# Loads of a decode kernel divided over two hardware DMA queues, SP's and ACT's

## The chip, the core and the metric

The kernel runs on one core of a Trainium2 chip. The metric is the device time of one execution in microseconds (us); the time before is the median of three runs. A core has TensorE (PE), VectorE (DVE), ScalarE (ACT), GpSimd (POOL) and SyncE (SP), which run their own instruction streams in order and meet through semaphores, and 16 DMA engines that move data between HBM and the on-chip memory. A load is issued by an instruction on one of the engines and joins the queue that belongs to this engine: SP's is named q1 in the profile, ACT's q10.

## The reference

One token passes through grouped-query attention with a long cache, and then through a small MLP block. B = S = 1, D = 512, 32 query heads, 8 key/value heads, 16,384 cached positions, head dimension 128; all in bfloat16.

```python
def _A_ref(x, k_cache, v_cache, wq, wo):
    q = heads(x @ wq)                      # 32 heads of 128
    k = jnp.repeat(k_cache, 4, axis=1)     # 8 groups, 4 query heads each
    v = jnp.repeat(v_cache, 4, axis=1)
    scores = jnp.einsum("bhqd,bhkd->bhqk", q, k) * (Dh ** -0.5)
    p = _softmax(scores, axis=-1)
    o = jnp.einsum("bhqk,bhkd->bhqd", p, v)
    return merge(o) @ wo

def _B_ref(x, w1, w2, w3, w4):
    ...
    x1 = x + hs                            # hs is zero with one position
    h2 = _gelu(_layernorm(x1, axis=-1) @ w3) @ w4
    return x1 + h2

h = x + _A_ref(_layernorm(x, axis=-1), A_k_cache, A_v_cache, A_wq, A_wo)
h2 = h + _B_ref(_layernorm(h, axis=-1), B_w1, B_w2, B_w3, B_w4)
return h2
```

In the MLP block the reference shifts four quarters of a hidden row by one or two positions, fills with zeros and multiplies by w2. With a single position nothing but zeros is left, so hs is zero and the kernel doesn't load w1 and w2: after the attention it normalises h, normalises that again for the product with w3, and adds h, the normalised h and the product with w4.

What must be read is 79.17 MB: wq and wo (4.19 MB each), K and V of 8 groups (4.19 MB each per group), w3 and w4 (1.84 MB each).

## The kernel before

The author's small scheduler (class `Program`) takes operations in program order, notes for each which keys it reads and writes, and derives the semaphore waits. It does not reorder: the order of calls is the order on each engine. So an operation that is added to an engine stands behind everything that was recorded for this engine earlier.

Positions are laid out with 128 rows of 128 positions, so one group's K is a tile of 128 partitions x 32 KB (`kb`, two buffers), and V comes as two halves of 8,192 positions, each 128 x 16 KB (`vb`, three buffers; the halves of the last group go to the first K buffer). wq and wo share one buffer (`wqo`), and w3 and w4 go to the second K buffer once the last keys have been read.

The main loop (L461) runs over g = 0 to 8 and works on the keys of group g and the values of group g-1:

- `transpose_keys` (L374): VectorE transposes the K tile in 8 pieces into `kt`. Every piece takes from both halves of each row, so it needs the whole row.
- `scores` (L384): TensorE multiplies `kt` by the queries into `s_ps`, in two halves.
- `values` (L439): TensorE multiplies the weights of group g-1 by the value halves into `O_ps`. It comes between the two halves of the scores and after them.
- `max_a`, `max_b`, `max_c` (L395 to L418): the row maximum, then ScalarE's two exponentials (L414).
- `weights` (L422): TensorE transposes the exponentials, VectorE copies them to `pt`. `gather` (L451): VectorE copies `O_ps` to `o_sb`, TensorE adds it up in `A_ps`.
- then the loads for later: `load_v(g, 0)`, `load_v(g, 1)`, and `load_k(g + 2)` (L490 to L494), and in the last group the pieces of wo, w3 and w4 (L495 to L504).

All these loads are issued by SP, which does nothing else; only x is issued by ACT. In the loop a load is recorded after the exponentials of its group, but on SP it waits only for its own buffer: `load_k(g + 2)` for the 8 transposes of group g, `load_v` for the products of the half that was in the buffer three halves earlier. wq, K0 and K1 are issued ahead of the loop, and the two halves of V0, whose buffers are free, stand right behind them on SP.

After the loop: the sums are normalised (L509 to L516), 32 x 4 products with wo give h (L522), `row_sums` and the inverse roots run on VectorE, 16 products with w3 (L535), Gelu on ScalarE (L542), a transpose, 56 products with w4 (L555), the final sum (L559) and the store.

The text calls the whole key tile of a group K0 to K7, and v00, v01, v10, ... the halves of the values (group, half); wo0, w30, w40 and so on are the pieces of the last weights, as the code names them.

Of the kernel before, what the change touches and what calls it, by code (L numbers as in the profile page):

```python
# [117 lines left out]
NCH = D // 128  # L118
FQ = FM // 4
NHC = FM // 128  # L120
WO = ((0, 14), (14, 28), (28, 32))
W3 = ((0, 3), (3, 4))
W4 = ((0, 10), (10, 14))
KRING = 2
VRING = 3
VT = 64 * DH
# [4 lines left out]
def bass_sequential_preLN__gqa_block_cached__mixer_s_mlp__decode_kernel(  # L131
# [13 lines left out]
    with ExitStack() as ctx:  # L145
        sb = lambda name, shape, dt: ctx.enter_context(nc.sbuf_tensor(name, shape, dt))
        ps = lambda name, shape, dt: ctx.enter_context(nc.psum_tensor(name, shape, dt))
        P = Program(nc, ctx)
# [10 lines left out]
        x4 = sb("x4", [4, 128], BF16)  # L159
# [39 lines left out]
        wqo = sb("wqo", [128, NCH * HQ * DH], BF16)  # L199
        kb = [sb(f"kb{i}", [128, 128 * DH], BF16) for i in range(KRING)]  # L200
        kt = sb("kt", [128, 128 * DH], BF16)
        vb = [sb(f"vb{i}", [128, VT], BF16) for i in range(VRING)]
        w3_sb = kb[1][:, 0:NCH * FM].rearrange("p (k f) -> p k f", k=NCH)
        w4_sb = kb[1][:, NCH * FM:2 * NCH * FM].rearrange("p (m c) -> p m c", m=NHC)
# [6 lines left out]
        m_ps, n_ps = mn_ps[:, 0:256], mn_ps[:, 256:512]  # L211


        def load(name, dst, src, key, by="SP", also=()):
            P.op(by, lambda e: e.dma_start(dst, src), w=[key, *also], dma=name)  # L215

        def load_k(g):
            i = g % KRING
            load(f"k{i}", kb[i][:, :], A_k_cache[0, g].rearrange("(p t) d -> p (t d)", p=128), ("k", i, 0),
                 also=[("k", i, n) for n in range(1, 4)])  # L220

        def value_tile(g, A):

            if g == HKV - 1:
                return kb[0][:, A * VT:(A + 1) * VT], ("k", 0, A)
            i = (2 * g + A) % VRING
            return vb[i][:, :], ("v", i)

        def load_v(g, A):
            src = A_v_cache[0, g, A * 8192:(A + 1) * 8192, :].rearrange("(p t) d -> p (t d)", p=128)  # L230
            dst, key = value_tile(g, A)
            load("v" + "_".join(map(str, key[1:])), dst, src, key)


        def dve(fn, r=(), w=(), bank=()):
            return P.op("DVE", fn, r, w, bank)
# [36 lines left out]
        def inverse_root(i, n):  # L273
# [17 lines left out]
            for k in range(3):  # L291
# [4 lines left out]
                    r=[(S, 8 + n), (T, n)], w=[key])  # L296


        load("x4", x4[:, :], A_x[0, 0:1, :].rearrange("o (q j) -> (o q) j", q=4), "x4", "ACT")
        load("wq", wqo[:, :], A_wq.rearrange("(p k) c -> p (k c)", k=NCH), ("wo", 0),  # L300
             also=[("wo", n) for n in range(1, len(WO))])
        load_k(0)
        load_k(1)

# [6 lines left out]
        for b in range(2):  # L311
            for e_ in range(2):
                n = 2 * b + e_
# [7 lines left out]
            r=["ident"], w=["quarter"])  # L321
# [7 lines left out]
            r=["hT", (("st", 0), 0), (("st", 0), 6)], w=["xn"])  # L329
# [3 lines left out]
            r=["selq_f"], w=["selq"])  # L333
        dve(lambda e: e.memset(nscale[:, :], -SCALE), w=["nscale"])
        act(lambda e: e.activation(scr[0:1, 0:1], mean4[0:1, 0:1], ACTF.Exp), r=["mean4"], w=["scr"])
        for i in range(2):
# [5 lines left out]
            r=["ident_f"], w=["row32"])  # L342
        dve(lambda e: e.tensor_reduce(row4[:, :], row32[:, :].rearrange("p (a u h) -> p u h a", a=4, u=2)[:, 0, :, :], AX.X, ALU.add),
            r=["row32"], w=["row4"])
        dve(lambda e: e.tensor_reduce(maskdd[:, :], ident_f[:, :].rearrange("p (n d) -> p d n", d=4), AX.X, ALU.add),
            r=["ident_f"], w=["maskdd"])
# [3 lines left out]
            r=["row32"], w=["zo"])  # L350
# [4 lines left out]
        for h in range(HQ):  # L355
            for k in range(NCH):
                pe(lambda e, h=h, k=k: e.matmul(n_ps[:, h:h + 1],  # L357
                                                wqo[:, k * HQ * DH + h * DH:k * HQ * DH + (h + 1) * DH],
                                                xn[:, k:k + 1], start=(k == 0), stop=(k == NCH - 1)),
                   r=["xn"] + [("wo", n) for n in range(len(WO))], w=["n"], bank=["mn"])  # L360
        dve(lambda e: e.tensor_copy(QT[:, :], n_ps[:, 0:HQ]), r=["n"], w=["QT"], bank=["mn"])
# [4 lines left out]
        for a in range(4):  # L366
            lo, hi = 32 * a, 32 * a + 32
# [6 lines left out]
        def transpose_keys(g, ts):  # L374
            i = g % KRING
            for t in ts:
                view = lambda x, t=t: x[:, :].bitcast(I32).rearrange("p (x l w) -> p x (l w)", x=2, l=64)[
                    :, :, t * 512:(t + 1) * 512]
                dve(lambda e, i=i, view=view: e.transpose(view(kt), view(kb[i])),  # L379
                    r=[("k", i, n) for n in range(4)], w=[("kt", t)])  # L380

        ktv = kt[:, :].rearrange("p (x l b s e) -> p b e l x s", x=2, l=64, b=2, s=32, e=2)

        def scores(g, half):  # L384
            for n in range(4):
                for ct in range(4):
                    c8 = 4 * half + ct
                    pe(lambda e, g=g, half=half, n=n, ct=ct, c8=c8: e.matmul(  # L388
                        s_ps[32 * ct:32 * ct + 32, half, :],
                        qb[:, n, g, :, :, :].rearrange("p a u h -> p (a u h)"),  # L390
                        ktv[:, n // 2, n % 2, 8 * c8:8 * c8 + 8, :, :],
                        start=(n == 0), stop=(n == 3)),
                       r=["qb", ("kt", c8)], w=[("s", half)], bank=[("s", half)])

        def max_a(half):  # L395
            dve(lambda e: e.tensor_reduce(mx[:, half:half + 1], s_ps[:, half, :], AX.X, ALU.max),  # L396
                r=[("s", half)], w=[("mx", half)], bank=[("s", half)])
# [41 lines left out]
        def values(g, A, qs):  # L439
            tile, key = value_tile(g, A)  # L440
            for q in qs:
                for ct in range(4):
                    n = 32 * (q // 2) + 8 * ct + 4 * (q % 2)
                    pe(lambda e, q=q, ct=ct, n=n: e.matmul(  # L444
                        O_ps[g % 2][32 * ct:32 * ct + 16, :],
                        pt[g % 2][:, ct, A, 4 * q:4 * q + 4, :].rearrange("p l h -> p (l h)"),
                        tile[:, n * DH:(n + 4) * DH],
                        start=(A == 0 and q == 0), stop=(A == 1 and q == 3)),
                       r=[key, ("pt", g % 2)], w=[("O", g % 2)], bank=[("O", g % 2)])
# [11 lines left out]
        for g in range(HKV + 1):  # L461
            if g < HKV:
                transpose_keys(g, range(3 if g == 1 else 0, 4))
                scores(g, 0)
                transpose_keys(g, range(4, 6))
                max_a(0)
                transpose_keys(g, range(6, 8))
            if g:
                values(g - 1, 0, range(4))
            if g < HKV:  # L470
                scores(g, 1)
                max_a(1)
            if g == 0:
                transpose_keys(1, range(0, 1))
            if g:
                values(g - 1, 1, range(2))
            if g < HKV:
                max_b()
            if g:
                values(g - 1, 1, range(2, 4))  # L480
            if g < HKV:
                max_c(g)
            if g == 0:
                transpose_keys(1, range(1, 3))
            if g < HKV:
                weights(g)
                denominator(g)
            if g:
                gather(g - 1)
            if g < HKV:  # L490
                for A in range(2):
                    load_v(g, A)
                if g + 2 < HKV:
                    load_k(g + 2)  # L494
            if g == HKV - 1:  # L495
                for n, (lo, hi) in enumerate(WO):
                    load(f"wo{n}", wqo[:, lo * D:hi * D], A_wo.rearrange("(p r) c -> p (r c)", p=128)[:, lo * D:hi * D],
                         ("wo", n))
                w3_in = B_w3.rearrange("(p k) f -> p k f", p=128)
                for n, (lo, hi) in enumerate(W3):  # L500
                    load(f"w3{n}", w3_sb[:, lo:hi, :], w3_in[:, lo:hi, :], ("k", 1, n))
                w4_in = B_w4.rearrange("(p m) c -> p m c", p=128)
                for n, (lo, hi) in enumerate(W4):
                    load(f"w4{n}", w4_sb[:, lo:hi, :], w4_in[:, lo:hi, :], ("k", 1, 2 + n))  # L504
                act(lambda e: e.activation(scr[0:1, 1:2], mean4[0:1, 0:1], ACTF.Gelu_apprx_tanh),
                    r=["mean4"], w=["scr"])

# [7 lines left out]
            r=["o_m"], w=["o_f"])  # L515
# [3 lines left out]
           r=["quarter", "x4"], w=[("O", 0)], bank=[("O", 0)])  # L519
        for r_ in range(32):  # L520
            for q in range(4):
                pe(lambda e, r_=r_, q=q: e.matmul(O_ps[0][32 * q:32 * q + 32, 0:128], copies(o_b[:, r_:r_ + 1], 32),  # L522
                                                  wqo[:, r_ * D + q * 128:r_ * D + (q + 1) * 128],
                                                  start=False, stop=(r_ == 31), skip_group_check=True),
                   r=["o_b", ("wo", piece(WO, r_))], w=[("O", 0)], bank=[("O", 0)])
        s = st[1]
# [3 lines left out]
            r=["hT", (S, 0)], w=["hc"])  # L530


        for k in range(NCH):
            for q in range(4):
                pe(lambda e, k=k, q=q: e.matmul(s_ps[32 * q:32 * q + 32, 0, 0:FQ], hc[:, k, :],  # L535
                                                w3_sb[:, k, q * FQ:(q + 1) * FQ], start=(k == 0), stop=(k == NCH - 1)),
                   r=["hc", ("k", 1, piece(W3, k))], w=[("s", 0)], bank=[("s", 0)])
        variance(1)
        inverse_root(1, 1)
        for n in range(2):  # L540
            lo, hi = n * NHC // 2, (n + 1) * NHC // 2
# [9 lines left out]
            r=["hr", (S, 0), (S, 6)], w=["xs"])  # L551
        dve(lambda e: e.tensor_tensor(xsum[:, :], hr[:, :], xs[:, :], ALU.add), r=["hr", "xs"], w=["xsum"])
        for m in range(NHC):
            for o in range(4):
                pe(lambda e, m=m, o=o: e.matmul(  # L555
                    n_ps[32 * o:32 * o + 32, 0:128], hcol[:, m, :], w4_sb[:, m, o * 128:(o + 1) * 128],
                    start=(m == 0), stop=(m == NHC - 1)),
                   r=[("hcol", 2 * m // NHC), ("k", 1, 2 + piece(W4, m))], w=["n"], bank=["mn"])
        dve(lambda e: e.tensor_tensor(fin[:, :], xsum[:, :], n_ps[:, 0:128], ALU.add),  # L559
            r=["n", "xsum"], w=["fin"], bank=["mn"])  # L560
        P.op("SP", lambda e: e.dma_start(out[0, 0:1, :].rearrange("o (q j) -> (o q) j", q=4), fin[0:128:32, :]),
             r=["fin"], w=["out"], dma="out")
# [32 lines left out]
```

## Time and profile before

| | us |
|---|---|
| time, median of three runs | 194.05 (194.0 to 194.56) |
| the profiled execution's own time | 194.11 |
| its span on the core | 192.3 |
| TensorE busy, of the span | 112.5 (58%) |
| VectorE busy | 122.0 (63%) |
| ScalarE busy | 16.9 (9%) |
| SP's queue waiting for TensorE (before it issues) | 93.4 |
| SP's queue waiting for VectorE | 54.6 |
| K, from issue to landing, median | 26.3 |
| V half, from issue to landing, median | 24.2 |

The span is what the profiler saw between the first and the last instruction of the core; the time also holds what lies around it. Busy time counts an engine's instructions without waits and without the issue of transfers. In the page's slices each digit is the busy share of a fortieth of the span in tenths, and the GB/s row below it is what all queues moved in that slice. In a timeline row the columns are start and duration in us, engine, line, operation, result and operands with partitions x elements, and count; the bracket gives the idle time of the engine before it and what ended it.

### The profile page before, as it was taken

The numbers are of one execution on the slowest core, as the hardware profiler recorded it, in microseconds if no ns is written. First come the engines' busy times: TensorE is split into PE (matmuls) and PEld (weight loads), VectorE is DVE, ScalarE is ACT, GpSimd is POOL, SyncE is SP. The second block draws the span as 40 slices with busy tenths as digits, with TensorE's granted clock in tenths as the row PEclk, the third lists the DMA queues.
The fourth block names the chain that finished last, engine by engine and source line by source line (L and its number), as shares of the span: only waits on it lengthen the run. The fifth ranks groups of instructions, "written<-read, shape, count | busy, mean of one in ns | idle before, by whom it ended". The sixth has DMA issues, their size and how long they took to land.

```text
span 192.3 us, 2624 instructions
## 1 busy us (share of the span) xinstructions
PE 112.5 (58%) x1106; PEld 56.3 (29%) x1106; DVE 122.0 (63%) x236; ACT 16.9 (9%) x38; POOL 3.3 (2%) x17
## 2 busy tenths in 40 slices
PE   1025046567837766774776558645885676594533
PEld 1025001242234235223422522242223422453402
DVE  5834099499449928964894379536944796403274
ACT  3000000030030030003000200030003000600010
POOL 2000000000000000000000000000000000000000
PEclk9999999999985695588559655975558559669555
DMA  6999999999999999999999999999999999999990
GB/s 225 429 436 433 436 436 426 423 455 436 395 429 467 436 388 429 460 423 409 426 436 436 419 423 436 443 426 416 450 441 399 416 429 436 417 421 424 421 376 34
DMA packets 4634, 79.32 MB, mean 412 GB/s; under 512 B 528, under 2 KB 528, under 8 KB 912
## 3 DMA queue, kind: packets, MB, share of 16 engines
q1 hardware_dynamic: 4616, 79.17, 96.8%
q8 instruction: 8, 0.13, 0.3%
q14 instruction: 2, 0.02, 0.0%
q10 hardware_dynamic: 8, 0.00, 0.0%
HBM read 79.17 MB, written 0.00 MB: 412 GB/s over the span
## 4 chain that ended last, share of the span: by engine, by line
DMA 47%; DVE 18%; issue 2%; PE 2%; SPq 1%; ACT 0%; DVEq 0%; ACTq 0%
DMA kb<-in_A_k_cache_dram 28%; DMA wqo<-in_A_wo_dram 19%; DVE kt L379 13%; PE O_ps L522 1%; DVE mx L396 1%; DVE st L293 1%; SPq L215 1%; DVE hcol L546 1%; DVE sti L295 0%; PE T_ps L424 0%; DVE pt L430 0%; PE mn_ps L260 0%; ACT hg L542 0%; DVE xs L550 0%; DVE st L295 0%
## 5 line engine op out<-in xcount | busy, mean ns | idle before, releaser
L379 DVE STREAM_TRANSPOSE kt<-kb 128x1024 int32<-128x1024 int32 x64 | 74.0, 1212 | 11.1 <-DMA kb<-in_A_k_cache_dram 11.0
L388 PE MATMUL s_ps<-kt,qb 128*32 128x512 bf16 x256 | 47.7, 557 | 32.0 <-DVE kt L379 32.0
L444 PE MATMUL O_ps<-vb,pt 128*16 128x512 bf16 x224 | 29.2, 533 | 0.0
L388 PEld LDWEIGHTS s_ps<-kt,qb 128*32 128x32 bf16 x256 | 10.7, 114 | 61.6 <-DVE kt L379 53.9
L414 ACT ACTIVATE p_sb<-s_ps,bias 128x512 bf16<-128x512 f32 x16 | 12.7, 822 | 149.9 <-PE mn_ps L408 113.8
L456 PE MATMUL A_ps<-o_sb,zo 128*128 128x128 f32 x64 | 15.7, 422 | 10.5 <-DVE o_sb L453 10.5
L430 DVE COPY pt<-T_ps 64x256 bf16<-64x256 bf16 (+2 forms) x40 | 9.8, 261 | 15.5 <-PE T_ps L424 15.2
L396 DVE TENSOR_REDUCE mx<-s_ps 128x1 f32<-128x512 f32 x16 | 10.8, 677 | 11.9 <-PE s_ps L388 9.8
L424 PE MATMUL T_ps<-ident,p_sb 128*128 128x128 bf16 x128 | 11.7, 249 | 11.0 <-ACT p_sb L414 11.0
L456 PEld LDWEIGHTS A_ps<-o_sb,zo 128*128 128x128 f32 x64 | 13.4, 311 | 11.6 <-DVE o_sb L453 11.6
L424 PEld LDWEIGHTS T_ps<-ident,p_sb 128*128 128x128 bf16 x128 | 8.8, 111 | 12.9 <-ACT p_sb L414 12.7
L444 PEld LDWEIGHTS O_ps<-vb,pt 128*16 128x16 bf16 x224 | 9.4, 115 | 10.0 <-issue 8.5
L357 PE MATMUL mn_ps<-xn,wqo 128*128 128x1 bf16 x128 | 3.6, 165 | 9.4 <-DMA wqo<-in_A_wq_dram 9.4
L401 PE MATMUL mn_ps<-ident_f,mx 128*1 128x128 f32 x32 | 7.3, 322 | 2.5 <-DVE mx L396 2.5
L453 DVE COPY o_sb<-O_ps 128x512 f32<-128x512 f32 x8 | 5.5, 692 | 5.0 <-PE O_ps L444 4.7
L357 PEld LDWEIGHTS mn_ps<-xn,wqo 128*128 128x128 bf16 x128 | 3.5, 104 | 9.4 <-issue 9.4
L404 DVE TENSOR_REDUCE nm<-mn_ps 1x4 f32<-1x256 f32 x8 | 3.3, 406 | 3.7 <-PE mn_ps L401 3.7
L522 PE MATMUL O_ps<-wqo,o_b 128*32 128x128 bf16 x128 | 3.1, 271 | 2.9 <-DMA wqo<-in_A_wo_dram 1.6
L420 POOL COPY p_sb<-p_sb 128x64 bf16<-128x64 bf16 x8 | 1.9, 237 | 160.5 <-ACT p_sb L414 160.5
L401 PEld LDWEIGHTS mn_ps<-ident_f,mx 128*1 128x1 f32 x32 | 2.3, 90 | 7.5 <-DVE mx L396 5.3
L408 PEld LDWEIGHTS mn_ps<-nm,nscale 1*128 1x128 f32 x16 | 2.5, 198 | 5.5 <-DVE nm L404 5.5
L408 PE MATMUL mn_ps<-nm,nscale 1*128 1x4 f32 x16 | 3.2, 270 | 1.2 <-DVE nm L404 0.9
(75 smaller groups left out, 51.7 us busy)
## 6 DMA issues: line engine op xcount, KB each, us to landing
kb<-in_A_k_cache_dram SPq DMA_DIRECT2D x8, 4096.0 KB, 26.3
vb<-in_A_v_cache_dram SPq DMA_DIRECT2D x14, 2048.0 KB, 24.2
wqo<-in_A_wq_dram SPq DMA_DIRECT2D x1, 4096.0 KB, 12.3
kb<-in_A_v_cache_dram SPq DMA_DIRECT2D x2, 2048.0 KB, 26.8
wqo<-in_A_wo_dram SPq DMA_DIRECT2D x2, 1792.0 KB, 34.7
kb<-in_B_w_dram SPq DMA_DIRECT2D x1, 1344.0 KB, 22.9
kb<-in_B_w_dram SPq DMA_DIRECT2D x1, 1280.0 KB, 26.2
wqo<-in_A_wo_dram SPq DMA_DIRECT2D x1, 512.0 KB, 37.4
```

Of the source, the lines that this page charges most:

```text
L357: pe(lambda e, h=h, k=k: e.matmul(n_ps[:, h:h + 1], wqo[:, k * HQ * DH + h * DH:k * HQ * DH + (h + 1) * DH], xn[:, k:k + 1], start=(k == 0 ...
L379: dve(lambda e, i=i, view=view: e.transpose(view(kt), view(kb[i])), r=[("k", i, n) for n in range(4)], w=[("kt", t)])
L388: pe(lambda e, g=g, half=half, n=n, ct=ct, c8=c8: e.matmul(s_ps[32 * ct:32 * ct + 32, half, :], qb[:, n, g, :, :, :].rearrange("p a u h -> ...
L396: dve(lambda e: e.tensor_reduce(mx[:, half:half + 1], s_ps[:, half, :], AX.X, ALU.max), r=[("s", half)], w=[("mx", half)], bank=[("s", half)])
L401: pe(lambda e, half=half: e.matmul(m_ps[0:1, half * 128:half * 128 + 128], mx[:, half:half + 1], ident_f[:, :], start=True, stop=True), r= ...
L408: pe(lambda e: e.matmul(n_ps[:, 0:REP], nscale[0:1, :], nm[0:1, :], start=True, stop=True), r=["nm", "nscale"], w=["n"], bank=["mn"])
L414: act(lambda e, half=half, g=g: e.activation(p_sb[:, half * 512:half * 512 + 512].rearrange("p (l s x) -> p l x s", l=8, x=2), s_ps[:, hal ...
L424: pe(lambda e, w=w: e.transpose(T_ps[:, w, :], p_sb[:, w * 64:w * 64 + 128], ident[:, :]), r=[("p", w // 8), ("p", (w + 1) // 8), "ident"] ...
L430: dve(lambda e, lo=lo, w0=w0, w1=w1, l0=l0: e.tensor_copy(to[lo:lo + 64, l0:l0 + w1 - w0, :, :], of[lo:lo + 64, w0:w1, :, lo // 64, 0, :]) ...
L444: pe(lambda e, q=q, ct=ct, n=n: e.matmul(O_ps[g % 2][32 * ct:32 * ct + 16, :], pt[g % 2][:, ct, A, 4 * q:4 * q + 4, :].rearrange("p l h -> ...
L453: dve(lambda e, g=g: e.tensor_copy(o_sb[g % 2][:, :], O_ps[g % 2][:, :]), r=[("O", g % 2)], w=[("osb", g % 2)], bank=[("O", g % 2)])
L456: pe(lambda e, g=g, j=j: e.matmul(A_ps[:, 0:128], zo[:, j, 112 - 16 * g:240 - 16 * g], o_sb[g % 2][:, j * 128:(j + 1) * 128], start=False, ...
```

## The change

Every load is given a queue: 0 is SP's, 1 is ACT's. A row of K or of wq is cut in the middle, SP loads the left halves and ACT the right halves. Of the values, SP loads half 0 and ACT half 1 of every group. The last weights are cut into an even number of pieces (wo 4 instead of 3, w3 two equal ones, w4 4 instead of 2) that go to the queues in turn. The keys by which the scheduler tells parts of a buffer apart grow from 4 to 6 for K. The calls stay where they were in program order; what computes is unchanged.

```diff
-WO = ((0, 14), (14, 28), (28, 32))
-W3 = ((0, 3), (3, 4))
-W4 = ((0, 10), (10, 14))
+WO = ((0, 14), (14, 28), (28, 30), (30, 32))
+W3 = ((0, 2), (2, 4))
+W4 = ((0, 5), (5, 10), (10, 12), (12, 14))
+QUEUES = ("SP", "ACT")
+KPARTS = 6
...
-        def load(name, dst, src, key, by="SP", also=()):
-            P.op(by, lambda e: e.dma_start(dst, src), w=[key, *also], dma=name)
+        def load(name, dst, src, key, by):
+            P.op(QUEUES[by], lambda e: e.dma_start(dst, src), w=[key], dma=name)
+
+        def load_rows(name, dst, src, keys):
+
+            n = dst.shape[1] // 2
+            for h in range(2):
+                P.op(QUEUES[h], lambda e, h=h: e.dma_start(dst[:, h * n:(h + 1) * n], src[:, h * n:(h + 1) * n]),
+                     w=keys[h::2], dma=f"{name}_{h}")
...
-            load(f"k{i}", kb[i][:, :], A_k_cache[0, g].rearrange("(p t) d -> p (t d)", p=128), ("k", i, 0),
-                 also=[("k", i, n) for n in range(1, 4)])
+            load_rows(f"k{i}", kb[i][:, :], A_k_cache[0, g].rearrange("(p t) d -> p (t d)", p=128),
+                      [("k", i, n) for n in range(KPARTS)])
...
-            load("v" + "_".join(map(str, key[1:])), dst, src, key)
+            load("v" + "_".join(map(str, key[1:])) + f"_{A}", dst, src, key, A)
...
-        load("wq", wqo[:, :], A_wq.rearrange("(p k) c -> p (k c)", k=NCH), ("wo", 0),
-             also=[("wo", n) for n in range(1, len(WO))])
+        load_rows("wq", wqo[:, :], A_wq.rearrange("(p k) c -> p (k c)", k=NCH), [("wo", n) for n in range(len(WO))])
...
-                         ("wo", n))
+                         ("wo", n), n % 2)
...
-                    load(f"w3{n}", w3_sb[:, lo:hi, :], w3_in[:, lo:hi, :], ("k", 1, n))
+                    load(f"w3{n}", w3_sb[:, lo:hi, :], w3_in[:, lo:hi, :], ("k", 1, n), n % 2)
...
-                    load(f"w4{n}", w4_sb[:, lo:hi, :], w4_in[:, lo:hi, :], ("k", 1, 2 + n))
+                    load(f"w4{n}", w4_sb[:, lo:hi, :], w4_in[:, lo:hi, :], ("k", 1, 2 + n), n % 2)
```

In the new kernel the lines move down by 8: the exponentials, L414 before, are L422, the transposes L387, the copy of the outputs L461.

More of the change, by code (lines that the diff above doesn't have):

```diff
@@ L296, in inverse_root @@
                     r=[(S, 8 + n), (T, n)], w=[key])
-        load("x4", x4[:, :], A_x[0, 0:1, :].rearrange("o (q j) -> (o q) j", q=4), "x4", "ACT")
-        load("wq", wqo[:, :], A_wq.rearrange("(p k) c -> p (k c)", k=NCH), ("wo", 0),
-             also=[("wo", n) for n in range(1, len(WO))])
+        load("x4", x4[:, :], A_x[0, 0:1, :].rearrange("o (q j) -> (o q) j", q=4), "x4", 1)
+        load_rows("wq", wqo[:, :], A_wq.rearrange("(p k) c -> p (k c)", k=NCH), [("wo", n) for n in range(len(WO))])
         load_k(0)
@@ L379, in transpose_keys @@
                 dve(lambda e, i=i, view=view: e.transpose(view(kt), view(kb[i])),
-                    r=[("k", i, n) for n in range(4)], w=[("kt", t)])
+                    r=[("k", i, n) for n in range(KPARTS)], w=[("kt", t)])
         ktv = kt[:, :].rearrange("p (x l b s e) -> p b e l x s", x=2, l=64, b=2, s=32, e=2)
```

## The prediction

> **What bounds the kernel now.** First the page's slices and queues, since the kernel reads 79 MB.
>
> ```profile
> DMA  6999999999999999999999999999999999999990
> GB/s 225 429 436 433 436 436 426 423 455 436 395 429 467 436 388 429 460 423 409 426 436 436 419 423 436 443 426 416 450 441 399 416 429 436 417 421 424 421 376 34
> ...
> q1 hardware_dynamic: 4616, 79.17, 96.8%
> ...
> q10 hardware_dynamic: 8, 0.00, 0.0%
> ...
> DMA 47%; DVE 18%; issue 2%; PE 2%; SPq 1%; ACT 0%; DVEq 0%; ACTq 0%
> ```
>
> The transfer engines are full from the first slice to the last but one: one queue, q1 (SP's), moves everything at 429 GB/s (mean of slices 2 to 37), and the chain of waits runs through transfers. q10 is ACT's, used once, for x. A value half (2.10 MB) takes 4.9 us, a whole K (4.19 MB) 9.75 us, a group (K and two value halves) 19.5 us. The packet records agree: a 32 KB packet has a median of 1,214 ns, a 16 KB one 613 ns, so a packet costs some 11 ns plus its bytes at 27.3 GB/s. The timeline, in order of time, says when loads are asked for and data is used:
>
> ```profile
> 39.72 0.82 ACT L414 ACTIVATE p_sb<-s_ps,bias 128x512 bf16<-128x512 f32 x1
> ...
> 57.40 6.87 DVE L379 STREAM_TRANSPOSE kt<-kb 128x1024 int32<-128x1024 int32 x6
> ...
> 131.29 6.88 DVE L379 STREAM_TRANSPOSE kt<-kb 128x1024 int32<-128x1024 int32 x6 [2.33 <-DMA kb<-in_A_k_cache_dram]
> ...
> 141.09 0.80 SPq L215 DMA_DIRECT2D kb<-in_A_v_cache_dram  x2
> ...
> 146.36 0.82 ACT L414 ACTIVATE p_sb<-s_ps,bias 128x512 bf16<-128x512 f32 x1
> ...
> 150.93 6.88 DVE L379 STREAM_TRANSPOSE kt<-kb 128x1024 int32<-128x1024 int32 x6 [1.37 <-DMA kb<-in_A_k_cache_dram]
> ...
> 164.93 0.82 ACT L414 ACTIVATE p_sb<-s_ps,bias 128x512 bf16<-128x512 f32 x1
> ...
> 173.15 0.69 DVE L453 COPY o_sb<-O_ps 128x512 f32<-128x512 f32 x1 [4.74 <-PE O_ps L444]
> ...
> 176.51 0.96 PE L522 MATMUL O_ps<-wqo,o_b 128*32 128x128 bf16 x56 [1.30 <-DVE o_b L516]
> ```
>
> Call S(g) the first transpose of group g. The keys are free at S+9.8 (131.29 to 141.09); the exponentials end at S+14.8 (150.93 to 165.75) or S+15.9 (131.29 to 147.18). Compute needs 18.3 us a group (the copy of o_sb ends at 149.56, from 131.29), 1.2 us less than the bytes, and waits 1.4 to 2.3 us for K. The last value half is asked for at 141.5 and, by the packet records, is down at 170.2, just as TensorE gets to it at 170.47. So compute is hidden under the stream and the tail fits its end: neither has two microseconds to spare.
>
> **The change, part by part.**
>
> *Where the requests stand.* The diff gives value half 1 of each group, half of each K, wo1, wo3, w31, w41 and w43 to ACT's queue. ACT works in order, and in its instruction order these stand behind the two exponentials of group g: v(g,1) and half of K(g+2) go out at S+15.4, not when their buffer is free; in the last group v(7,1) and five weight pieces. SP asks for its half of K(g+2) at S+9.8 as now and then for v(g+1,0). The waits on ACT name its own earlier loads of the same buffer, consumed long ago: none costs anything. Queued behind ACT's issues are the next exponentials, 14 us later (two issues at about 0.4 us each, by SP's 0.80 for two), and in the last group the Gelu table load (1.28 us), which ends near 180 for a Gelu needed near 194; uncovered it would cost 4 us.
>
> *The lag.* No row shows two busy queues. I let the 16 engines alternate packets between them (equal halves; the bounds follow), and give one queue everything while the other is empty. A piece of 2.10 MB takes 9.8 us shared, 4.9 alone. Data starts 1.5 us after its issue: wq is issued at 0.74, and 225 GB/s in a slice of 4.81 us at 430 means a start at 2.3.
> Call K2a the half of K2 that SP loads and K2b the half that ACT loads. Both queues bring wq, K0, K1 by 33.9 (the first transpose starts at 24.01 on a wait for K0; plus 9.75, and 0.2 for smaller packets). SP goes on alone: v00 to 38.8, then K2a (asked for at 33.98). ACT is empty: its v01 was asked for at 2 us before; now it follows the first exponentials (40.6 plus 0.2) and moves from 42.3. K2a ends at 45.0, v01 at 52.1, v10 at 54.9, K2b at 61.9, and by then SP is 7 us into K3a (asked for at 49.09). So S(2) is 62.1 against 57.40. Afterwards both queues stay fed: ACT's pair is asked for at S+15.4, data from S+16.9, while its K(g+1)b still runs to S+19.4; SP's K(g+2)a can move from S+11.3, while SP's value half runs to S+12.4. So a group takes the bytes' 19.6 us, and S(7) = 62.1 + 5 x 19.6 = 160.1, 9.2 behind 150.93. In bytes it is the same lag: SP is ahead by v60 and most of v70, 3.8 MB that came after K7. The bounds: if ACT's packets always went first, K2b would end at 42.3 + 9.8 = 52.1, in time for 57.4 (rival 1); if SP's did, K3a and v20 would pass ahead of it (v10 to 48.6, v01 until K3a's data starts at 50.6, K3a and v20 to 60.4, the rest of v01 to 63.3) and K2b end at 68.2, 6.3 later (the size of rival 2).
>
> *Packets.* K and wq rows become two of 16 KB: 1,152 more packets x 12 ns / 16 = 0.9 us; the finer weight pieces 384 x 11 ns / 16 = 0.3; 12 more transfers, each with a semaphore packet of 9 ns on every engine, 0.1. Together 1.3, inside the times above. What changing queues costs at a packet, no row shows: from minus 11 ns (the fixed cost hides behind the other queue, 350 packets an engine, -3.9 us) to plus 20 ns (another fixed cost and a semaphore packet's 9 ns, +7 us). I take 0, between the two.
>
> *The tail.* v61 moves from 159.9 to 169.7 beside v70 (to 162.7) and wo0, wo2 (2.10 MB, to 171.1). SP's w30, w40, w42 (1.83 MB) wait for the transposes of group 7, 160.1 + 9.8, and end at 175.7. ACT's exponentials end at 160.1 + 15.4 = 175.5: the stream runs dry until v(7,1) moves, alone, from 177.0 to 181.9, then wo1 and wo3 (2.10 MB) to 186.8 and the rest to 191.1. Now v(7,1) decides: 0.2 for its signal, 1.3 for its 16 products (half of 32 in 2.62 us), 3.4 to the output product (173.15 to 176.51): 186.8. wo1, wo3 are there at 187.0. The 128 products take 3.1 (0.96 for 56, 2.11 for 72): 189.9. From their end to the span's end now: 192.3 - 181.24 = 11.1, which also covers the last weights. Sum: span 201.0, with 1.8 around it (194.11 against 192.3) **202.8 us**, +8.7; the median of the runs, 194.05, is the profiled run's time.
>
> The engines' DMA share is 1.00 to 1.01 in the windows 60-80 and 100-120 us on one queue. The Trainium skill, "DMA: Bandwidth & Descriptors", section "Issuing engines are not separate DMA queues", says that DMAs from several engines run on the same 16 engines and that issuing from two saves sequencer time only; the trace agrees, since SP's issues (0.33 us) lie under the 24.2 and 26.3 us that value halves and keys take from issue to landing. By it alone the change would be worth nothing but its packets, 195.4 (rival 4). The same page, "Queues, rings and completion order", has each engine go round-robin over its queues by packet; no run here has two busy queues yet; by it the sum is the 202.8 above.
>
> **The rivals.**
> 1. *Only the tail is late.* K's order does not suffer, S(7) stays 150.9, exponentials end at 165.8. v(7,1) moves from 167.3, shared with SP's rest (2.5 MB), to 177.1; wo1, wo3 to 182.9; output product 182.0 to 185.2; span 196.3, time 198.1. For it: K was asked for 24 us ahead, much to hide in. Against: the walk from 42 us on.
> 2. *A larger lag: changing queues costs.* +20 ns on some 320 packets an engine before v(7,1): +6.4, 209.2. For it: both queues would be busy nearly always. Against: a semaphore packet of 4 bytes between data packets of one queue costs only its 9 ns.
> 3. *Faster: one queue does not fill an engine, two do.* Place: every packet; 27.3 GB/s would be the queue's rate. At 7% more, compute bounds the group (18.3): S(7) = 57.4 + 5 x 18.3 = 148.9, exponentials 164.3, v(7,1) 165.8 to 170.4, then 0.2 + 1.3 + 3.4 + 3.1 + 11.1: 189.5, time 191.3. Between 0% (202.8) and 7% that is 1.6 us a percent; it decides from some 5.3% on. Against: engines busy without gaps, packets of one size within 1%.
> 4. *The queues act as one stream and the lag is absorbed:* 194.1 + 1.3 = 195.4. Against: v(7,1) cannot be asked for before 165.8.
>
> **How the numbers follow.** Forecast 60%, rival 1 15%, rival 2 13%, rival 3 8%, rival 4 4%. 0.3% (0.6 us) is what a measurement here tells from no change. Faster: rival 3, 0.08. Same: half of rival 4, 0.02. Slower: 0.90. The likeliest case's own range is 199 (fixed cost hidden) to 206. The range, 197.5 to 208, adds rival 1 and the lower part of rival 2, and leaves out rivals 3 and 4 and a part of 2.
>
> **What would show it.** q10 with near half the bytes. First transposes near 62 us in group 2 and 160 in group 7, and groups 19.6 us apart, waiting for K each time; ACT's issues right behind L422's exponentials; a slice below 350 GB/s near 176; the last values' products ending near 183 on a wait for a transfer. Wrong, if group 7 starts near 151 (rival 1), if 16 KB packets are slower than 613 ns with the engines full (rival 2), or if slices pass 450 GB/s throughout (rival 3).

## The result and the profile after

The changed kernel takes 206.63 us (median of 4 runs, 205.56 to 206.69) against 194.15 before: a ratio of 1.062, 95% interval 1.0601 to 1.0639. Forecast were 202.8 us, in a range from 197.5 to 208. The span of the profiled execution is 204.9 us instead of 192.3.

The page of the kernel after: busy share of the transfer engines and GB/s in 40 slices of 5.12 us, the queues, and the chain that ended last.

```profile
DMA  6999999899999999999999999999999997999400
GB/s 243 422 435 435 419 438 419 294 427 435 419 441 419 432 432 416 438 419 435 432 413 441 422 422 445 409 441 425 416 440 416 434 423 252 428 410 411 186 0 0
...
q1 hardware_dynamic: 3176, 39.59, 46.4%
q10 hardware_dynamic: 3176, 39.59, 45.6%
...
DMA 59%; DVE 24%; PE 11%; issue 4%; ACT 1%; ACTq 0%; DVEq 0%
```

Each queue moved half of the bytes, and where there is work the rate is that of one queue before: 427 GB/s in slices 2 to 37 without the two dips, against 429. But slice 8 (36 to 41 us) fell to 294 GB/s and slice 34 (169 to 174 us) to 252, and the last two slices carry nothing: bytes that could have moved earlier were not asked for, and the work after the last of them is longer.

The timeline of the kernel after (start and duration in us; the bracket is the idle time of the engine before and its cause):

```profile
26.47 6.88 DVE L387 STREAM_TRANSPOSE kt<-kb 128x1024 int32<-128x1024 int32 x6 [4.89 <-DMA kb<-in_A_k_cache_dram]
...
64.78 6.88 DVE L387 STREAM_TRANSPOSE kt<-kb 128x1024 int32<-128x1024 int32 x6 [2.04 <-DMA kb<-in_A_k_cache_dram]
...
161.44 6.88 DVE L387 STREAM_TRANSPOSE kt<-kb 128x1024 int32<-128x1024 int32 x6 [2.12 <-DMA kb<-in_A_k_cache_dram]
...
174.63 0.82 ACT L422 ACTIVATE p_sb<-s_ps,bias 128x512 bf16<-128x512 f32 x1 [17.94 <-PE mn_ps L416]
174.74 0.33 ACTq L217 DMA_DIRECT2D kb<-in_A_v_cache_dram  x1
...
184.38 1.88 PE L452 MATMUL O_ps<-kb,pt 128*16 128x512 bf16 x16 [1.72 <-DMA kb<-in_A_v_cache_dram]
186.32 0.69 DVE L461 COPY o_sb<-O_ps 128x512 f32<-128x512 f32 x1 [7.60 <-PE O_ps L452]
```

Group 0 started at 26.5 (24.0 before), group 2 at 64.8 (57.4) and group 7 at 161.4 (150.9). The issue of v(7,1) stands a tenth of a microsecond behind the start of the group's first exponential, and the last products of the values wait for it until 184.4. The copy of their result is at 186.32 instead of 173.15; 12.6 us is what the span lost in all.

### The profile page after: what moved, and what is told of

It reads as the page before. It is cut to its first block, busy times and chain, and to the rows that moved or that the text cites. A ratio compares the mean times of both kernels' runs of the same rounds, so it can differ in the third digit from the quotient of the medians.

```text
span 204.9 us, 2638 instructions
## 1 busy us (share of the span) xinstructions
PE 116.0 (57%) x1106; PEld 58.9 (29%) x1106; DVE 122.3 (60%) x236; ACT 16.9 (8%) x38; POOL 3.3 (2%) x17
## 4 chain that ended last, share of the span: by engine, by line
DMA 59%; DVE 24%; PE 11%; issue 4%; ACT 1%; ACTq 0%; DVEq 0%
DMA kb<-in_A_k_cache_dram 48%; DVE kt L387 17%; DMA vb<-in_A_v_cache_dram 7%; DMA kb<-in_A_v_cache_dram 5%; PE O_ps L452 3%; PE s_ps L396 3%; DVE mx L404 2%; PE O_ps L530 2%; PE mn_ps L416 1%; PE A_ps L464 1%; PE mn_ps L409 1%; DVE st L302 1%; ACT p_sb L422 1%; DVE nm L412 1%; DVE hcol L554 1%
## 5 line engine op out<-in xcount | busy, mean ns | idle before, releaser
L387 DVE STREAM_TRANSPOSE kt<-kb 128x1024 int32<-128x1024 int32 x64 | 74.1, 1212 | 16.1 <-DMA kb<-in_A_k_cache_dram 16.1
L396 PEld LDWEIGHTS s_ps<-kt,qb 128*32 128x32 bf16 x256 | 10.6, 112 | 66.5 <-DVE kt L387 59.7
L422 ACT ACTIVATE p_sb<-s_ps,bias 128x512 bf16<-128x512 f32 x16 | 12.7, 823 | 158.8 <-PE mn_ps L416 121.8
L464 PE MATMUL A_ps<-o_sb,zo 128*128 128x128 f32 x64 | 16.6, 441 | 9.9 <-DVE o_sb L461 9.9
L432 PE MATMUL T_ps<-ident,p_sb 128*128 128x128 bf16 x128 | 12.7, 264 | 10.8 <-ACT p_sb L422 10.8
L464 PEld LDWEIGHTS A_ps<-o_sb,zo 128*128 128x128 f32 x64 | 14.3, 328 | 11.4 <-DVE o_sb L461 11.4
L432 PEld LDWEIGHTS T_ps<-ident,p_sb 128*128 128x128 bf16 x128 | 9.6, 118 | 12.7 <-ACT p_sb L422 12.5
L461 DVE COPY o_sb<-O_ps 128x512 f32<-128x512 f32 x8 | 5.5, 691 | 7.8 <-PE O_ps L452 7.6
L452 PE MATMUL O_ps<-kb,pt 128*16 128x512 bf16 x32 | 3.8, 623 | 1.7 <-DMA kb<-in_A_v_cache_dram 1.7
```

Of the source, the lines that this page charges most:

```text
L396: pe(lambda e, g=g, half=half, n=n, ct=ct, c8=c8: e.matmul(s_ps[32 * ct:32 * ct + 32, half, :], qb[:, n, g, :, :, :].rearrange("p a u h -> ...
L422: act(lambda e, half=half, g=g: e.activation(p_sb[:, half * 512:half * 512 + 512].rearrange("p (l s x) -> p l x s", l=8, x=2), s_ps[:, hal ...
L432: pe(lambda e, w=w: e.transpose(T_ps[:, w, :], p_sb[:, w * 64:w * 64 + 128], ident[:, :]), r=[("p", w // 8), ("p", (w + 1) // 8), "ident"] ...
L452: pe(lambda e, q=q, ct=ct, n=n: e.matmul(O_ps[g % 2][32 * ct:32 * ct + 16, :], pt[g % 2][:, ct, A, 4 * q:4 * q + 4, :].rearrange("p l h -> ...
L461: dve(lambda e, g=g: e.tensor_copy(o_sb[g % 2][:, :], O_ps[g % 2][:, :]), r=[("O", g % 2)], w=[("osb", g % 2)], bank=[("O", g % 2)])
L464: pe(lambda e, g=g, j=j: e.matmul(A_ps[:, 0:128], zo[:, j, 112 - 16 * g:240 - 16 * g], o_sb[g % 2][:, j * 128:(j + 1) * 128], start=False, ...
```

## The experiments

Times are medians; ratios are to the kernel before in the same comparison (194.2 to 194.3 us), with 95% intervals. "Early" means that a load on ACT is recorded ahead of its group's exponentials; v(7,1), wo1 and wo3 are then recorded one group sooner still, ahead of those of group 6.

**All requests early.** Queues and pieces as in the changed kernel; only the place in ACT's order changes. Helpers that load one queue's share (`hs`, `load_wo(h)`, `load_w34(h)`) and the calls that then load SP's share of the last weights in their old place are left out of the diff.

```diff
                 scores(g, 1)
                 max_a(1)
+                if g < HKV - 1:
+                    load_v(g, 1)
+                if g + 2 < HKV:
+                    load_k(g + 2, (1,))
+                if g == HKV - 2:
+                    load_v(HKV - 1, 1)
+                    load_wo(1)
+                if g == HKV - 1:
+                    load_w34(1)
...
-                for A in range(2):
-                    load_v(g, A)
+                load_v(g, 0)
                 if g + 2 < HKV:
-                    load_k(g + 2)
+                    load_k(g + 2, (0,))
```

> Both queues carry exactly what they carry in the changed kernel, but every load on ACT's queue is put ahead of its group's exponentials in ACT's order, so that it waits for its buffer alone, as on SP. Theory (the requests come late because they stand behind the exponentials): group 7 starts near 153 us instead of 161, the last value half is down before TensorE wants it, the stream does not run dry, and the time is 195 to 198 us. Rival (two busy queues cost by themselves, by switching, smaller packets or uneven halves): group 7 stays near 160 and the time at 203 to 207 us.

Measured: 195.89 us, ratio 1.0109 (1.0056 to 1.0161). Its page and its timeline:

```profile
GB/s 220 429 433 433 426 433 429 429 433 421 422 429 429 422 426 422 429 433 433 433 422 429 429 429 426 426 422 426 426 427 417 433 433 429 425 426 402 418 347 7
...
q1 hardware_dynamic: 3176, 39.59, 48.5%
q10 hardware_dynamic: 3176, 39.59, 48.2%
```

```profile
144.34 0.35 ACTq L217 DMA_DIRECT2D kb<-in_A_v_cache_dram  x1
...
147.68 0.82 ACT L422 ACTIVATE p_sb<-s_ps,bias 128x512 bf16<-128x512 f32 x1 [16.96 <-DVE nmh L418]
...
154.10 6.88 DVE L387 STREAM_TRANSPOSE kt<-kb 128x1024 int32<-128x1024 int32 x6 [2.16 <-DMA kb<-in_A_k_cache_dram]
...
176.67 0.69 DVE L461 COPY o_sb<-O_ps 128x512 f32<-128x512 f32 x1 [5.08 <-PE O_ps L452]
```

The same two queues with the same bytes; the dips are gone, v(7,1) is asked for 30 us earlier than in the changed kernel (144.34 against 174.74), and group 7 starts at 154.1. Of the 12.5 us lost, 10.7 come from where the requests stand.

**One queue, cut loads.**

```diff
-QUEUES = ("SP", "ACT")
+QUEUES = ("SP", "SP")
```

> All loads go to SP's queue, cut as in the changed kernel into halves of rows and more pieces. Theory: only the packets' fixed cost is left, 194.1 + 1.3 = 195.4 us, 195 to 196. Rival (smaller packets and finer pieces are what costs): 199 us or more.

Measured: 195.51 us, ratio 1.0063 (1.0048 to 1.0078). So cutting rows and pieces costs 1.2 us, as summed from the packets. The kernel with two queues and early requests lies 0.4 us above this one, but the intervals of the two overlap, so that a cost of the second queue by itself is not shown.

**Late tail taken away.** Only the last group's value half and the last weights move to SP.

```diff
-            load("v" + "_".join(map(str, key[1:])) + f"_{A}", dst, src, key, A)
+            load("v" + "_".join(map(str, key[1:])) + f"_{A}", dst, src, key, A if g < HKV - 1 else 0)
...
-                         ("wo", n), n % 2)
+                         ("wo", n), 0)
...
-                    load(f"w3{n}", w3_sb[:, lo:hi, :], w3_in[:, lo:hi, :], ("k", 1, n), n % 2)
+                    load(f"w3{n}", w3_sb[:, lo:hi, :], w3_in[:, lo:hi, :], ("k", 1, n), 0)
...
-                    load(f"w4{n}", w4_sb[:, lo:hi, :], w4_in[:, lo:hi, :], ("k", 1, 2 + n), n % 2)
+                    load(f"w4{n}", w4_sb[:, lo:hi, :], w4_in[:, lo:hi, :], ("k", 1, 2 + n), 0)
```

> The changed kernel, but the last group's second value half and all pieces of the last weights are asked for by SP. Theory (lag of K and late tail add up): group 7 still starts near 161 us, no transfer is waited for in the last values, and the time falls by 1.7 to 3.5 us, to 203 to 205. Rival (the tail alone is late): 197 to 199 us. Rival (the lag alone is late): no change, 206 to 207 us.

Measured: 202.03 us, ratio 1.0409 (1.0366 to 1.0452). The timeline of this kernel:

```profile
161.13 6.88 DVE L387 STREAM_TRANSPOSE kt<-kb 128x1024 int32<-128x1024 int32 x6 [2.11 <-DMA kb<-in_A_k_cache_dram]
...
183.93 0.69 DVE L461 COPY o_sb<-O_ps 128x512 f32<-128x512 f32 x1 [5.66 <-PE O_ps L452]
```

Group 7 starts as late as in the changed kernel, and yet 4.6 us are saved, a microsecond more than expected. The four runs lie far apart (201.39 to 203.47), and the profiled one is the longest of them. Both rivals fall: the time is neither that of a late tail alone nor that of a lag alone.

**Late tail alone.** The early kernel again, with ACT's loads of the last group put back behind the exponentials.

```diff
-                if g == HKV - 2:
-                    load_v(HKV - 1, 1)
-                    load_wo(1)
-                if g == HKV - 1:
-                    load_w34(1)
...
-                load_wo(0)
-                load_w34(0)
+                load_v(g, 1)
+                for h in range(2):
+                    load_wo(h)
+                    load_w34(h)
```

> The kernel with early requests, except that in the last group ACT's loads (second value half and its pieces of the last weights) stand behind the exponentials again. Theory (lag and late tail add up): group 7 starts near 154 us as with all requests early, its last value half is waited for, and the time is 199 to 201.5 us, so that the tail is worth 4 to 5 us on top of early requests as it was on top of late ones. Rival (one hides the other): 196 or 204 us.

Measured: 201.85 us, ratio 1.0411 (1.038 to 1.0442): 0.35 above the bounds of the theory. Its timeline, and the line of its waits (total, times, longest) for the last values:

```profile
153.97 6.88 DVE L387 STREAM_TRANSPOSE kt<-kb 128x1024 int32<-128x1024 int32 x6 [2.46 <-DMA kb<-in_A_k_cache_dram]
...
167.30 0.33 ACTq L217 DMA_DIRECT2D kb<-in_A_v_cache_dram  x1
...
181.32 0.69 DVE L461 COPY o_sb<-O_ps 128x512 f32<-128x512 f32 x1 [9.87 <-PE O_ps L452]
```

```profile
PE O_ps L452 <- DMA kb<-in_A_v_cache_dram: 4.0, 1, 4.0
```

Group 7 starts at 153.97, v(7,1) is asked for at 167.30, TensorE waits 4.0 us for it, and the last copy of outputs, at 181.32, waits for these products. So the late tail is worth 6.0 us on early requests and 4.6 on late ones. The late requests of the other groups are worth 6.1 us by themselves (202.03 against 195.89), and both together 10.7: the two overlap by 1.4 us.

**v01 ahead of the loop.** One load less that stands behind exponentials.

```diff
+        load_v(0, 1)
         for g in range(HKV + 1):
...
-                for A in range(2):
+                for A in range(1 if g == 0 else 2):
```

> The changed kernel, but ACT asks for the second value half of group 0 ahead of the loop, as SP does in the kernel before; every later load on ACT stays behind its exponentials. Theory (every group's request is late): group 2 starts near 60 us instead of 64.8, but the lag comes back group by group, group 7 starts at 158 to 161, time 203 to 206 us. Rival (the queues fell out of step once, when ACT's queue was empty near 35 to 45 us): group 7 starts near 153 and the time is 198 to 200 us.

Measured: 205.00 us, ratio 1.0529 (1.0476 to 1.0582). Its timeline:

```profile
60.36 6.86 DVE L387 STREAM_TRANSPOSE kt<-kb 128x1024 int32<-128x1024 int32 x6
...
80.47 6.88 DVE L387 STREAM_TRANSPOSE kt<-kb 128x1024 int32<-128x1024 int32 x6 [2.90 <-DMA kb<-in_A_k_cache_dram]
...
159.12 6.88 DVE L387 STREAM_TRANSPOSE kt<-kb 128x1024 int32<-128x1024 int32 x6 [2.69 <-DMA kb<-in_A_k_cache_dram]
```

Group 2 does not wait for its keys any more, group 3 does again, by 2.9 us, and at group 7 only 2.3 us of the gain in group 2 (4.4) are left. Against the kernel before, group 2 is 3.0 us late here, group 3 is 6.0 and groups 4 to 7 are 7.8 to 8.2 us late; in the changed kernel it is 7.4, 8.7 and 10.4 to 10.6. So the lag isn't one slip of v01: it builds up to group 4 and is then carried along, since from there the groups follow one another at 19.6 us (19.9 once), the pace of their bytes.

**The keys alone, the values alone.** First only wq and the keys on two queues: values to SP with `key, 0)` in `load_v`, the last weights with 0 for `n % 2`.

> Only wq and the keys are divided over the two queues; both value halves and all last weights are asked for by SP. ACT's halves of the keys still stand behind the exponentials. Theory (the lag is bytes of other tiles that pass ahead of a K because ACT carries two pieces a group, both asked for late): ACT now has one piece a group and is done with it long before it is wanted, group 7 starts at 152 to 154 us, time 195.5 to 197.5. Rival (a divided K is late by itself): group 7 near 160, time 202 us or more.

Measured: 197.63 us, ratio 1.0158 (1.0126 to 1.019), just past the upper bound. Group 7 starts at 154.52, and after group 0 no group waits for keys. TensorE's weight loads wait 8.0 us for values instead:

```profile
PEld O_ps L452 <- DMA vb<-in_A_v_cache_dram: 8.0, 5, 3.0
```

I put this down to the halves of keys that ACT now brings beside values which are used before them. The trace fits, since ACT's half of K7 is down at 144.5, ten microseconds before group 7 starts, but it was not tried by itself.

Then only the values and the last weights on two queues:

```diff
-                P.op(QUEUES[h], lambda e, h=h: e.dma_start(dst[:, h * n:(h + 1) * n], src[:, h * n:(h + 1) * n]),
+                P.op(QUEUES[0], lambda e, h=h: e.dma_start(dst[:, h * n:(h + 1) * n], src[:, h * n:(h + 1) * n]),
```

> Keys and wq are cut in halves as in the changed kernel, but both halves go to SP; ACT keeps its value halves and its pieces of the last weights, behind the exponentials. Theory: no lag of the keys (group 7 starts at 151 to 154 us), but the tail is late: the last value half is asked for 13.3 us after the start of group 7 and shares the engines with SP's pieces, time 198.5 to 201.5. Rival (any late request on ACT makes the keys lag): group 7 near 160, time 204 us or more.

Measured: 202.43 us, ratio 1.0415 (1.0392 to 1.0437). Group 7 starts at 152.44 as the theory has it, but the time is 0.9 past its bound. TensorE's weight loads wait 4.5 us for v(7,1) and 12.8 us for values of the groups ahead of it:

```profile
PEld O_ps L452 <- DMA vb<-in_A_v_cache_dram: 12.8, 5, 4.6
...
PEld O_ps L452 <- DMA kb<-in_A_v_cache_dram: 4.5, 1, 4.5
```

The sum for this kernel had only v(7,1) late; the values of other groups are late too.

**Who is first in line.** The early kernel with the load of x on SP: `"x4", 0)` instead of `"x4", 1)`.

> The kernel with early requests, with the load of x moved from ACT's queue to SP's, so that ACT issues its half of wq first. In the changed kernel ACT's first wq packet started 4.4 us after its issue, SP's 1.3 us after its own. If the queue that issues second has to wait for packets of the other that the engines have already taken, SP's half of wq now starts 4 us after its issue and ACT's 1.3; if ACT's queue is slow by itself, ACT's still starts 4 us after its issue. In both cases the first keys stay 2 to 3 us late (26 to 27 us) and the time near 195.9.

Measured once, 195.44 us. SP's and ACT's issues at the start, first of the changed kernel, then of this one:

```profile
0.74 0.39 SPq L223 DMA_DIRECT2D wqo<-in_A_wq_dram  x1
...
1.33 0.36 ACTq L223 DMA_DIRECT2D wqo<-in_A_wq_dram  x1
```

```profile
0.74 0.38 ACTq L223 DMA_DIRECT2D wqo<-in_A_wq_dram  x1
...
1.18 0.36 SPq L223 DMA_DIRECT2D wqo<-in_A_wq_dram  x1
```

By the packet records, in the time of these rows, the first half of wq started to move at 1.75 on SP and the second at 5.46 on ACT in the changed kernel; here ACT's started at 1.79 and SP's at 5.61. That is 1.0 and 4.1 us after the issue in the one kernel, 1.0 and 4.4 in the other (the expectation's 1.3 and 4.4 are both a quarter of a microsecond too long). The delay goes with the place in line and not with the engine. The keys of group 0 are there at 26.59, as in the other kernels with two queues at the start.

**Whole rows, early requests.** Packets and start as before the change: K, wq and v(g,0) whole on SP, group 0 on SP alone, v(g,1) and every other piece of the last weights early on ACT.

```diff
-W4 = ((0, 5), (5, 10), (10, 12), (12, 14))
+W4 = ((0, 7), (7, 14))
...
-            load_rows(f"k{i}", kb[i][:, :], A_k_cache[0, g].rearrange("(p t) d -> p (t d)", p=128),
-                      [("k", i, n) for n in range(KPARTS)])
+            load(f"k{i}", kb[i][:, :], A_k_cache[0, g].rearrange("(p t) d -> p (t d)", p=128), ("k", i, 0), 0,
+                 also=[("k", i, n) for n in range(1, KPARTS)])
```

> Whole rows and as few pieces as before (w4 in two equal ones), keys and half 0 of the values on SP, half 1 and every other piece of the last weights on ACT, asked for ahead of the exponentials; group 0 comes over SP alone. Packets and start are those of the kernel before. Theory (two queues neither cost nor give anything once the requests are early): 194.3 us, 193.7 to 195. Rival (a second queue gives bandwidth or hides fixed costs): under 193. Rival (switching costs): over 196.

Measured: 197.52 us, ratio 1.0168 (1.0145 to 1.0192). The expectation was wrong by 3 us. The timeline of this kernel:

```profile
143.59 0.40 ACTq L217 DMA_DIRECT2D kb<-in_A_v_cache_dram  x1
...
153.31 6.88 DVE L388 STREAM_TRANSPOSE kt<-kb 128x1024 int32<-128x1024 int32 x6 [1.98 <-DMA kb<-in_A_k_cache_dram]
...
163.13 1.88 PE L453 MATMUL O_ps<-vb,pt 128*16 128x512 bf16 x16 [3.25 <-DMA vb<-in_A_v_cache_dram]
```

TensorE waits 3.25 us for v60, the first value half of group 6. By the packet records v61 started to move at 146.7 and v71 at 157.5 on ACT's queue, beside K7 and v60 on SP's. By the semaphores that a load raises when it has landed, K7 was down at 153.3, v61 at 159.2 and v60, which is used ahead of v61, only at 163.1; before the change it was K7 at 150.9, v60 at 155.8 and v61 at 160.7. ACT's queue had a quarter of the bytes and ran ahead. Asking early isn't enough, then: two queues can also lose the order of use.

**The same, with the last group on SP.** ACT keeps nothing but v(g,1) of groups 1 to 6.

```diff
-            load("v" + "_".join(map(str, key[1:])) + f"_{A}", dst, src, key, A if g else 0)
+            load("v" + "_".join(map(str, key[1:])) + f"_{A}", dst, src, key, A if 0 < g < HKV - 1 else 0)
```

> The kernel with whole rows and early requests, but the last group's second value half and all last weights come over SP in the order in which they are used; ACT has nothing but value half 1 of groups 1 to 6. That kernel took 197.5 instead of 194.3; by its packet records ACT's queue, with a quarter of the bytes, ran ahead: v61, v71 and wo1 moved beside K7, v60 and v70, which are used first. Theory (order alone costs): the first values of group 7 are waited for by less than 1 us instead of 3.3, and the time is 195 to 196.5 us. Rival (mixing 32 KB and 16 KB packets or switching queues costs): 197 to 198 us.

Measured: 194.68 us, ratio 1.0036 (1.0008 to 1.0064). That is a little below the theory's range. It has mixed packets and two queues for most of the stream, and takes 2.8 us less than the kernel with the last group on both. The wait for v60 is 1.17 us, a little over the forecast. Switching queues or mixing packets is not what cost the 3 us (the interval here leaves it 1.2 us at most); bringing bytes ahead of those needed first is. v60 is down at 160.8 here. Group 7 starts 2.2 us later than before the change (153.15), and the span is only 0.6 longer: before the change the tail had waited 1.65 us for a piece of wo anyway.

None of these kernels beats the one before.

## Why the prediction was right

- *What bounds the kernel.* Right: with requests in time (all early with equal shares, or one queue) the stream moves at its old rate and the time is that of the bytes. Rival 3, that two queues fill an engine better, falls: no slice of the early kernel passes 433 GB/s. What the Trainium skill, "DMA: Bandwidth & Descriptors", section "Issuing engines are not separate DMA queues", states, that the loads of all issuing engines run on the same 16 DMA engines, is borne out: 195.51 us on one queue, 195.89 on two.
- *Where the requests stand.* Right in cause, off in size: they go out 13.3 us after the group's first transpose (161.44 to 174.74), not 15.4. The prediction had them wait for the end of the second exponential (176.22); the issue follows the start of the first one by 0.11 us.
- *The lag.* Group 2 was forecast at 62.1 and came at 64.78, group 7 at 160.1 and came at 161.44; group 3 follows group 2 after 18.35 us, and from there on groups are 19.6 us apart, as forecast. What I missed is that a queue that starts while the other fills the engines starts late: 1.5 us were put in for any load, and ACT's first data came 4.1 us after its issue at the start and 3.4 us in group 0 (issue 41.52, data 44.92). v01 was to move from 42.3, so it was 2.6 us late, and that is nearly the whole error of group 2 (2.7). Group 0 started 2.5 us later than before (26.47 against 24.01), where I had put in 0.2 at most. Equal shares held: from K4's half (102.6) to K7's (161.3) ACT's pieces landed 9.8 us apart, as put in for a shared piece.
- *Packets.* Right: 1.3 forecast, 1.2 measured with one queue. Changing queues costs nothing that shows: the median 16 KB packet takes 612 ns with two queues, 613 before, and rival 2 falls.
- *The tail.* Right in cause. The stream did run dry, but near 170 to 173 us instead of 176, since SP's pieces waited for group 7 while ACT had nothing; v(7,1) then started to move at 177.0, beside SP's last piece, and was there at 184.4, 22.9 us after the group's start, where 22.0 were forecast (160.1 to 182.1). That these are so near is in part luck: against the group's start it was asked for 2.1 us sooner than forecast, its first data came 0.8 us later after the issue, and it took 7.4 us from the first data to the landing instead of 5.1; why so long is open. From there to the output product TensorE and VectorE took 6.2 us, against 4.7 put in from the kernel before. The same products took longer, first before the change and then after it:

```profile
173.90 1.16 PE L456 MATMUL A_ps<-o_sb,zo 128*128 128x128 f32 x8 [0.81 <-DVE o_sb L453]
```

```profile
187.07 2.08 PE L464 MATMUL A_ps<-o_sb,zo 128*128 128x128 f32 x8 [0.80 <-DVE o_sb L461]
```

The clock granted to TensorE was 1.00 in the first row and 0.50 in the second. The prediction took these times over from the kernel before without asking for the clock; that the clock is the cause fits the direction and most of the ratio (1.8), but no run changes it by itself.

- *The sum.* Its span was 201.0, measured are 204.9. Of the 3.9 us, group 7 accounts for 1.3, v(7,1) for 0.9, the way to the output product for 1.5 and its products for 0.3 (3.4 instead of 3.1); the way from there to the end was 0.1 shorter.
- *The rivals.* Rival 1 (the tail alone) gave 198.1 with the keys in time; a kernel with just that takes 201.85, and the changed one has the lag as well. Rival 4 (one stream, lag absorbed) is what one gets with the requests moved, 195.89, not with the change as it is.

Put together: 194.3 before, 1.2 for cut loads, 0.4 (not clear of the spread) for two queues with early requests, 6.0 for the late tail, 4.8 for the late requests of the other groups: 206.7. These are the steps from one measured kernel to the next, so the sum must come out; taken in the other order the late requests of the other groups are worth 6.1 and the late tail 4.6.

## What to carry to other kernels

Where the transfer engines were full, as here, a second queue brought no rate and changed only the order of bytes, and where the order moved away from the order of use by more than the waits could hide, it was paid for. A load put on the queue of an engine that also computes is asked for when this engine's program gets there, not when its buffer is free: look at what stands ahead of it. And check the queue with less to carry, since here it ran ahead and took the engines from what was wanted next, even when all requests were early.

## What the runs showed of the hardware

- A queue that starts while the other is already full waits: at the start its first packets moved 4.1 us (ACT second, issue 1.33, data 5.46) or 4.4 us (SP second, issue 1.18, data 5.61) after their issue, against 1.0 us for the queue that is first. Later in the stream it was 3.4 to 3.6 us each time that ACT's queue started empty beside a full one: beside 16 KB packets (v01 to v61 in the kernel with only the values on two queues) as beside 32 KB ones (v11 to v61 in the kernel with whole rows). In that time the other queue had five to six of the first started on each engine, but under three of the second. So it is not a fixed number of packets; what sets it is not shown.
- A load's issue on ACT does not wait for the exponentials ahead of it to end: it came 0.11 us after the first had started and 0.66 us before the second started.
